# The second mixture by one level of Strassen's method, VectorE for its sums, explicit orders, and new attention orders

## The chip, the cores and the metric

The kernel runs on one core of a Trainium2 chip. Such a core has five engines that work side by side from their own queues: TensorE (PE: matmuls, with PEld for the loads of stationary tiles), VectorE (DVE), ScalarE (ACT), GpSimd (POOL) and SyncE (SP, here only an issuer of transfers). Matmuls write to PSUM, the rest lies in SBUF or in DRAM. The metric is the device time of one execution in microseconds.

## What is computed

Four batches (B) of 576 tokens (S), 8 heads of 64. Causal attention with a bias from a cumulative sum goes into a first mixture (a gated MLP with a spatial matrix over the tokens), and that into a second one. The second is what the change touches most.

```python
def _moe2_ref(x, mu_k, mu_r, w_k, w_v, w_r):
    x_prev = np.concatenate([np.zeros((B, 1, D)), x[:, :-1, :]], axis=1)
    xk = mu_k * x + (1.0 - mu_k) * x_prev
    xr = mu_r * x + (1.0 - mu_r) * x_prev
    k = np.maximum(xk @ w_k, 0.0)            # 512 -> 1024
    v = k * k @ w_v                          # 1024 -> 512
    r = 1.0 / (1.0 + np.exp(-(xr @ w_r)))    # 512 -> 512
    return r * v

x = attention(q, k, v, s)                    # (4, 576, 512)
h = np.maximum(x @ w_in, 0.0); u, v = h[..., :512], h[..., 512:]
gated = u * (einsum('ts,bsd->btd', w_spatial, normalize(v)) + b_spatial)
x = gated @ w_out
return _moe2_ref(x, ...)
```

The weights come as float64 and are turned into float32 on the chip.

## The kernel before

All large matmuls work on operands that are split into a high part (rounded to fp32r by a copy) and the rest (a subtraction), and take three passes into the same PSUM tile, high by high, high by rest and rest by high: the helper `three`, whose matmuls have the line L703. A split therefore costs a copy (often ScalarE, L105; on GpSimd L108, on VectorE L102) and a subtraction (L120).

*Weights.* A queue of 64 jobs decodes one tile of 128x256 each, in parts that orders name one by one: dL loads, dF (ScalarE, L132 and L133), dD (VectorE, L138 to L143, and an add on GpSimd, L145), dT (high copy on ScalarE, rest on GpSimd, into a buffer `hl`), dS stores the pair to DRAM. Fetches bring whole matrices back.

*Attention.* Sixteen pairs of heads are worked as a pipeline of steps; START is the written order of the beginning, ORDER that of each of 13 steps, TAIL1 and TAIL2 that of the end, where the first gate of mixture 1 begins. A name in them is one small piece: `xh` is the high copy of a step's queries and keys (64x1152), `s` the scores (L405), whose maxima VectorE takes (L411), `e` the transposed scores and exponentials (L443, L463), after which GpSimd cuts the diagonal (selects, L467), `a` and `b` the product with v (L501 to L505), whose sums go through DRAM and come back as `rb` to scale the output (L538).

*Mixture 1* per batch: gate u, the spatial product (L788 with `ws`, the split spatial matrix), the next batch's gate v with its normalization, projection. Vector work is put behind by `later` and `tick`, and decode steps are strewn between.

*Mixture 2* runs over 6 chunks of 384 tokens. `mix` makes the shifted mixture (VectorE L723 and L725, split by L728 and L729). `ffk` makes 8 tiles of 128 features by 384 tokens, 12 matmuls each (4 blocks of the contraction by three passes); ScalarE takes Relu out of PSUM (L983), VectorE squares (L986), ScalarE makes the high part (L987), GpSimd the rest (L990). `ffr` is the gate, three tiles of 128 tokens by 512 with 12 matmuls each; ScalarE takes exp of the negative, VectorE adds one (L1005) and takes the reciprocal (L1006). `ffv` has three tiles of 128 tokens by 512 with 24 matmuls each (the very last is done as two of 256); VectorE multiplies by the gate out of PSUM (L1018), and the tile is stored.

## Time and profile before

| | |
|---|---|
| median of 3 runs | 687.47 us (685.01 to 688.98) |
| profiled execution, span | 684.9 us |
| TensorE busy | 650.0 us, 95% of the span |
| VectorE, ScalarE, GpSimd busy | 504.3, 375.6, 341.8 us |
| granted TensorE clock, mean | 0.993 |

The span is the time from the first to the last instruction of the profiled execution, to which the views below belong; it lies 2.6 us under the median of the runs. Busy times are sums over the instructions of an engine. A matmul's shown time reaches to its modelled end, beyond the start of the next, so what a matmul costs is read from the distances between starts. What ended an idle time stands behind an arrow. The granted clock is a share of 2.4 GHz, 0.5 being 1.2 GHz.

### The profile page before, as it was taken

To read this page: it belongs to the slowest core of one execution; us is meant where nothing else is said; L and a number is where in the kernel's file an instruction comes from. 1 tells how busy PE (TensorE), PEld (TensorE's weight loads), DVE (VectorE), ACT (ScalarE), POOL (GpSimd) and SP (SyncE) were. 2 spreads that over 40 slices of the span, in tenths; PEclk is the share of its full clock that TensorE was granted. 3 is DMA by queue.
4 is the path that set the end of the run, shared out by engine and by line. 5 is a ranking of instruction groups with operands and counts; after the bars stand their busy time and mean duration, and the time that the engine had idled before them with its cause. 6 is when DMAs were issued, how large, how long until landed. Compare 5 with 4: busy or idle time off the path is not lost.

```text
span 684.9 us, 10966 instructions
## 1 busy us (share of the span) xinstructions
PE 650.0 (95%) x3640; PEld 558.0 (81%) x3640; DVE 504.3 (74%) x1038; ACT 375.6 (55%) x824; POOL 341.8 (50%) x490
## 2 busy tenths in 40 slices
PE   2599999999999979999999999999999999999998
PEld 1476666666757968998999999988989898898987
DVE  6878887878853687768858754479596877959773
ACT  5599999999975474575565453331423323142330
POOL 4445656565674646566567555442434344244430
PEclk9999999999999989999999999999999999999999
DMA  6645556564458627562364572721001010000101
GB/s 180 131 107 151 156 144 161 143 164 128 123 158 264 210 72 222 158 198 94 101 208 146 150 260 84 258 111 47 0 1 47 0 47 1 31 17 1 46 1 47
DMA packets 65065, 78.23 MB, mean 114 GB/s; under 512 B 28763, under 2 KB 45563, under 8 KB 64496
## 3 DMA queue, kind: packets, MB, share of 16 engines
q1 hardware_dynamic: 63674, 75.81, 37.0%
q10 hardware_dynamic: 1334, 1.72, 1.0%
q8 instruction: 28, 0.46, 0.3%
q14 instruction: 29, 0.24, 0.1%
...
## 4 chain that ended last, share of the span: by engine, by line
PE 78%; DMA 9%; ACT 7%; DVE 4%; issue 1%; POOL 0%; ACTq 0%; SPq 0%; DVEq 0%
PE mm L703 57%; PE mm L788 8%; PE pv L505 4%; DMA r<-pt 3%; PE ps L443 3%; DMA qk<-in_qk_dram 2%; ACT big L105 2%; ACT pt L516 2%; PE pv L502 2%; DMA rd<-r 1%; PE s L405 1%; ACT e L463 1%; PE pv L501 1%; DVE jk L411 1%; DMA big<-augd 1%
## 5 line engine op out<-in xcount | busy, mean ns | idle before, releaser
L703 PE MATMUL mm<-big 128*128 128x384 f32 (+2 forms) x1176 | 202.5, 332 | 0.0
L703 PEld LDWEIGHTS mm<-big 128*128 128x128 f32 x1176 | 191.3, 188 | 8.6
L703 PE MATMUL mm<-w,vb 128*128 128x512 f32 (+1 forms) x304 | 90.4, 381 | 0.0
L986 DVE TENSOR_TENSOR r<-r 128x384 f32<-128x384 f32 x48 | 53.7, 1119 | 46.6 <-ACT r L983 46.6
L443 PE MATMUL ps<-big 128*128 128x288 f32 (+3 forms) x320 | 84.0, 362 | 1.7 <-ACT e L463 0.8
L405 PE MATMUL s<-big 128*128 128x288 f32 (+3 forms) x192 | 61.9, 378 | 20.4 <-POOL big L108 12.3
L145 POOL TENSOR_TENSOR f<-f,raw 128x256 int32<-128x256 int32 x64 | 53.4, 834 | 43.9 <-DVE f L143 33.7
L411 DVE CUSTOM_DVE_ANT_0 jk<-s,mask 128x288 bf16<-128x288 f32 (+4 forms) x160 | 61.9, 429 | 16.2 <-PE s L405 13.9
L467 POOL TENSOR_SCALAR_AFFINE_SELECT e<-e 128x128 f32<-128x128 f32 x128 | 52.4, 419 | 42.0 <-ACT e L463 37.2
L443 PEld LDWEIGHTS ps<-big 128*128 128x128 f32 x320 | 55.3, 197 | 19.8 <-issue 12.1
L405 PEld LDWEIGHTS s<-big 128*128 128x128 f32 x192 | 36.3, 206 | 36.6 <-DVE mx L411 12.6
L463 ACT ACTIVATE e<-ps 128x288 f32<-128x288 f32 (+3 forms) x160 | 60.6, 418 | 8.5 <-PE ps L443 7.1
L703 PEld LDWEIGHTS mm<-w,vb 128*128 128x128 f32 x304 | 56.0, 188 | 11.2
L788 PE MATMUL mm<-ws,vb 128*128 128x288 f32 x384 | 59.3, 303 | 4.6 <-DVE ws L120 2.6
L505 PE MATMUL pv<-e,vp 128*65 128x448 f32 (+2 forms) x192 | 63.5, 436 | 0.0
L1006 DVE RECIPROCAL rr<-rr 128x512 f32<-128x512 f32 x18 | 60.4, 3353 | 0.6
L788 PEld LDWEIGHTS mm<-ws,vb 128*128 128x128 f32 x384 | 54.8, 194 | 5.6 <-DVE ws L120 3.4
L987 ACT CAST vb<-r 128x384 fp32r<-128x384 f32 x48 | 24.7, 515 | 56.9 <-DVE r L986 56.9
L729 POOL TENSOR_TENSOR gh<-mix,vb 128x384 fp32r<-128x384 f32 x24 | 25.5, 1070 | 52.3 <-ACT vb L728 49.7
L703 PE MATMUL mm<-gh,wo 128*128 128x288 f32 x256 | 51.3, 294 | 0.0
L729 POOL TENSOR_TENSOR big<-mix,big 128x384 fp32r<-128x384 f32 x24 | 25.9, 1083 | 47.4 <-ACT big L728 38.7
L120 DVE TENSOR_TENSOR big<-qk,big 64x1152 fp32r<-64x1152 f32 (+1 forms) x37 | 44.3, 1201 | 6.1 <-ACT big L105 4.9
...
## 6 DMA issues: line engine op xcount, KB each, us to landing
...
```

The source lines that it names most:

```text
L145: nc.gpsimd.tensor_tensor(out=f, in0=f, in1=low, op=ALU.add)
L405: nc.tensor.matmul(out=ps[:, 0:kn], lhsT=W[g][:, h, 128 * i:128 * i + 128], rhs=X[g][:, x0:x0 + kn], start=True, stop=True,)
L411: nc.vector.tensor_tensor_reduce(out=jk[r0:128, 0:kn], in0=ps[r0:128, 0:kn], in1=mask[r0:128, m0:m0 + kn], scale=1.0, scalar=(dst if mid e ...
L443: nc.tensor.matmul(out=ps[:, o:o + b - a], lhsT=st[g][:, key0(h, 128 * j):key0(h, 128 * j) + 128], rhs=mv[g][:, h, 64 + a:64 + b], start=( ...
L463: nc.scalar.activation(out=e[:, o:o + n], in_=ps[:, 0:n], func=ACTF.Exp, scale=scale)
L467: nc.gpsimd.affine_select(out=d, in_=d, pattern=[[1, w]], base=0, channel_multiplier=-1, compare_op=ALU.is_ge, fill=0.0,)
L505: nc.tensor.matmul(out=pv[0:VW, 1, 448 - w:448], lhsT=lt, rhs=e[:, OFF[j]:OFF[j] + w] if j < 4 else es[p][:, w * h:w * h + w], start=False ...
L703: nc.tensor.matmul(out=ps, lhsT=x, rhs=y, start=(m == 0), stop=(m == n - 1))
L729: nc.gpsimd.tensor_tensor(out=dst[1][:, kc, :], in0=t, in1=dst[0][:, kc, :].bitcast(F32), op=ALU.subtract)
L788: nc.tensor.matmul(out=o, lhsT=x[:, sc, dd], rhs=y[:, sc, t], start=(sc == 0 and m == 0), stop=False)
L986: nc.vector.tensor_tensor(out=r, in0=r, in1=r, op=ALU.mult)
L1006: nc.vector.reciprocal(out=r, in_=r)
```

## The change

Both layers of the second mixture, `ffk` and `ffv`, are computed by one level of Strassen's method in Winograd's form: operands are taken as 2x2 blocks, of which four sums are made on the token side, and seven products of blocks take the place of eight. The sums of the weights are made once while decoding: four blocks of a weight give seven forms (`dC`: three subtractions on VectorE and one on GpSimd), each split and stored, so that there are 88 splits and stores instead of 64, and seven forms of 1 MB per weight are fetched.

The first layer works per batch on halves of 288 tokens and in chains of two feature tiles (8 chains of 7 products of 12 matmuls of 288 columns, per tile 6). The second works on 9 chunks of 256 tokens (7 products of 12 matmuls of 256 columns). Products add up in PSUM: bank X takes P1, P6, P7, P4 one upon the other, Y takes P5 and P3, Z takes P2. After P1, P6 and P7 ScalarE copies X out, before the next product is added to it; the results C11, C12, C22 are the sum of such a copy and another bank, by VectorE (with Relu in the first layer), C21 is X itself. The first layer's results are squared (mostly ScalarE), stored to DRAM and loaded again for the second. The gate takes ScalarE's Sigmoid in place of exp, add and reciprocal, and needs a second activation table for it.

Orders are written out for all of this (M0 to M3 for mixture 1 with its decode parts, K_ORDER, K_LAST, V_ORDER), in place of `later` and `tick`. START, ORDER, TAIL1 and TAIL2 are new. In attention, the `xh` copy and the high copy of a weight go from ScalarE to GpSimd; in mixture 1 the latter is ScalarE's, and 13 of the 32 rests L796 go from GpSimd to VectorE. Of the issuers, q of pair 0 (`ldq0`) and k of pair 1 (`ldk1`) go from ScalarE to SP, one transfer (`Mb`) from SP to ScalarE. The ring of split weights has 4 buffers instead of 2.

```diff
-    START = """ldk0 ldq0 lds ldk1 cx0 mask cw0 sums 0xh0 bases cx1 ldq1 sums2 0wh0 0ul0 dL 0wh1 rx00 dL 0ul1 augd pads0
...
+    START = """lds cx0 ldk0 cw0 dL tiny 0xh0 mask sums ldq0 ldq1 dL bases pads1 sums2 pads0 1wh1 ldk1 cx1 0wh0 rx00
...
+    def dec_combine(group, to):
+
+        b11, b12, b21, b22 = group
+        t2, t3, t4 = (tsp.tile([128, WN], F32, tag="ts", name="ts") for _ in range(3))
+        subtract(ENGINE["c3"], out=t3, in0=b22, in1=b12)
+        subtract(ENGINE["c1"], out=b12, in0=b12, in1=b11)
+        subtract(ENGINE["c2"], out=t2, in0=b22, in1=b12)
+        subtract(ENGINE["c4"], out=t4, in0=b21, in1=t2)
...
+    PROD = dict(P1=("A11", "B11", "X"), P5=("S1", "T1", "Y"), P6=("S2", "T2", "X"), P2=("A12", "B21", "Z"),
+                P7=("S3", "T3", "X"), P4=("A22", "T4", "X"), P3=("S4", "B22", "Y"))
+    COPY_OF = {"P1": "p1", "P6": "u2", "P7": "u3"}
+    SUM_OF = {"C11": ("Z", "p1"), "C22": ("Y", "u3"), "C21": ("X", None), "C12": ("Y", "u2")}
...
+    def product(ch, nm, j, n, pairs):
+
+        w, bank = PROD[nm][1:]
+        if nm in ("P1", "P2", "P5"):
+            ch[bank, j] = mm_tile()[:, 0:n]
+        ps = ch[bank, j]
+        m, last_m = 0, 3 * len(pairs) - 1
+        for (ah, al), (bh, bl) in pairs:
+            for x, y in ((ah, bh), (ah, bl), (al, bh)):
+                nc.tensor.matmul(out=ps, lhsT=x, rhs=y, start=(m == 0 and nm in ("P1", "P2", "P5")),
+                                 stop=(m == last_m), skip_group_check=True)
+                m += 1
...
+        def keep(nm, j):
+            u = COPY_OF[nm]
+            ch[u, j] = KC.take()
+            nc.scalar.copy(KC.items[ch[u, j]], ch["X", j])
+
+        def give(c, j):
+            bank, u = SUM_OF[c]
+            k = ch[c, j] = KO.take()
+            o, ps = KO.items[k], ch[bank, j]
+            if u is None:
+                nc.scalar.activation(out=o, in_=ps, func=ACTF.Relu)
+                return
+            nc.vector._custom_dve(TENSOR_ADD_SAT, out=o, in0=ps, in1=KC.items[ch[u, j]], s0=float("inf"), s1=0.0)
+            KC.free[ch[u, j]] = True
...
+        def add(q):
+            bank, u = SUM_OF[q]
+            ch[q] = VO.take()
+            nc.vector.tensor_tensor(out=VO.items[ch[q]], in0=ch[bank, 0], in1=VC.items[ch[u]], op=ALU.add)
+            VC.free[ch[u]] = True
...
+        def sig(i):
+            RS[c, i] = RT.take()
+            nc.scalar.activation(out=RT.items[RS[c, i]], in_=ops["ps", i], func=ACTF.Sigmoid)
...
-        r = bt.tile([128, 512], F32, tag="vr", name="rr")
-        nc.scalar.activation(out=r, in_=ps, func=ACTF.Exp, scale=-1.0)
-
-        def sig():
-            nc.vector.tensor_scalar(out=r, in0=r, scalar1=1.0, scalar2=None, op0=ALU.add)
-            nc.vector.reciprocal(out=r, in_=r)
...
+    V_ORDER = """sa3 xp1 ncH n+1 xP5 sa0 n+3 ru0 xP6 xu2 n+2 xP2 ncS ncA x+C11 xP7 xu3 nsA sa2 n+4 sd3 rg0 x+C22 ru1
...
```

ScalarE's queue in one attention step, before (CAST rows of `big` are the splits of queries and keys, `hl0` is the high part of a weight, `e` the exponentials, `pt` the output out of PSUM):

```order
L105 CAST big_73<-qk0_137 64x2x576
L463 ACTIVATE e_1279<-ps_1280 128x288
L105 CAST big_73<-qk0_137 64x1152
L105 CAST hl0_85<-f_1153 128x256
L463 ACTIVATE e_1279<-ps_1295 128x288
L105 CAST big_73<-big_73 64x1152
L463 ACTIVATE e_1279<-ps_1323 128x448
L516 ACTIVATE pt_1337<-pv_1287,eps_142 65x576
L463 ACTIVATE e_1279<-ps_1339 128x192
L463 ACTIVATE e_1344<-ps_1345 128x288
L463 ACTIVATE e_1279<-ps_1356 128x320
L105 CAST big_73<-big_73 64x2x576
```

and after:

```order
L106 CAST big_73<-qk1_151 64x2x576
L518 ACTIVATE e_1442<-ps_1443 128x288
L518 ACTIVATE e_1442<-ps_1450 128x288
L518 ACTIVATE e_1442<-ps_1466 128x192
L518 ACTIVATE e_1480<-ps_1481 128x288
L106 CAST big_73<-big_73 64x1152
L518 ACTIVATE e_1442<-ps_1494 128x320
L571 ACTIVATE pt_1504<-pv_1462,eps_155 65x576
L518 ACTIVATE e_1442<-ps_1506 128x448
L106 CAST big_73<-big_73 64x2x576
L518 ACTIVATE e_1480<-ps_1530 128x192
```

Of the four copies of queries and keys three are left, the one from the loaded `qk` as 64x1152 is gone, and so is `hl`.

GpSimd's queue in one step, before (AFFINE_SELECT cuts the diagonal of `e`, L538 scales an output, L120 and L145 belong to the weight decode):

```order
L467 AFFINE_SELECT e_1279<-e_1279 128x128 x2
L467 AFFINE_SELECT e_1344<-e_1344 128x128
L467 AFFINE_SELECT e_1279<-e_1279 128x128
L467 AFFINE_SELECT e_1344<-e_1344 128x128 x2
L538 TENSOR_TENSOR x1_72<-pt_1171,rb_1304 64x576
L481 AFFINE_SELECT e4_1410<-e4_1410 128x128
L484 MEMSET e4_1410 64x64
L467 AFFINE_SELECT e_1344<-e_1344 128x128
L467 AFFINE_SELECT e_1445<-e_1445 128x128
L120 TENSOR_TENSOR hl1_86<-f_1319,hl1_86 128x256
```

and after:

```order
L109 TENSOR_SCALAR hl1_86<-f_1182 128x256
L121 TENSOR_TENSOR hl1_86<-f_1182,hl1_86 128x256
L522 AFFINE_SELECT e_1276<-e_1276 128x128 x2
L109 TENSOR_SCALAR big_73<-qk0_150 64x1152
L522 AFFINE_SELECT e_1314<-e_1314 128x128
L522 AFFINE_SELECT e_1276<-e_1276 128x128 x2
L147 TENSOR_TENSOR f_1348<-f_1348,raw_840 128x256
L593 TENSOR_TENSOR x1_72<-pt_1173,rb_1327 64x576
L522 AFFINE_SELECT e_1314<-e_1314 128x128 x3
```

The two copies stand here now: `hl1` ahead of its own subtraction, `qk` between two selects.

TensorE at the beginning of mixture 2, after (`mm` with a number is a PSUM tile; a chain's bank X is 5758 and 5765, Y 5772 and 5779, Z 5802 and 5809; `big` are the weights' forms, `xs` and `vb` the token side):

```order
L987 MATMUL mm_5758<-xs_5605,big_73 128x288 x6
L987 MATMUL mm_5765<-xs_5605,big_73 128x288 x6
L987 MATMUL mm_5772<-xs_5605,big_73 128x288 x6
L987 MATMUL mm_5779<-xs_5605,big_73 128x288 x6
L987 MATMUL mm_5758<-xs_5605,big_73 128x288 x6
L987 MATMUL mm_5765<-xs_5605,big_73 128x288 x6
L987 MATMUL mm_5802<-vb_2770,big_73 128x288 x6
L987 MATMUL mm_5809<-vb_2770,big_73 128x288 x6
L987 MATMUL mm_5758<-vb_2770,big_73 128x288 x6
L987 MATMUL mm_5765<-vb_2770,big_73 128x288 x6
L987 MATMUL mm_5841<-xs_5605,big_73 128x288 x6
L987 MATMUL mm_5848<-xs_5605,big_73 128x288 x6
```

The products are P1, P5, P6, P2, P7 and the next chain's P1: between two products into bank X there is one of another bank or chain. Before, eight tiles of 12 matmuls of 384 columns followed one another, each in a PSUM tile of its own.

VectorE in the second layer, before (L986 squares, `mix` rows make the mixtures, L1005 and L1006 the gate; a part of a chunk of 384 tokens):

```order
L986 TENSOR_TENSOR r<-r 128x384 x8
L723 TENSOR_SCALAR mix<-x_72,small 128x384
L725 SCALAR_TENSOR_TENSOR mix<-x_72,small,mix 128x384
L1005 TENSOR_SCALAR rr<-rr 128x512
L1006 RECIPROCAL rr<-rr 128x512
L723 TENSOR_SCALAR mix<-x_72,small 128x384
L725 SCALAR_TENSOR_TENSOR mix<-x_72,small,mix 128x384
L1005 TENSOR_SCALAR rr<-rr 128x512
```

and after, one chunk of 256 tokens (L959 from `vf` are sums and rests, L1141 adds out of PSUM, L1150 and the rows into `rt` multiply by the gate, L1176 mixes):

```order
L959 TENSOR_TENSOR vf<-vf 128x512 x3
L1141 TENSOR_TENSOR vf<-mm,vf 128x256
L959 TENSOR_TENSOR gl<-vf,gl 128x1024
L959 TENSOR_TENSOR vf<-vf 128x512
L1176 SCALAR_TENSOR_TENSOR hl_86<-x_72,small,hl_86 128x256
L1141 TENSOR_TENSOR vf<-mm,vf 128x256
L1176 SCALAR_TENSOR_TENSOR hl_86<-x_72,small,hl_86 128x256
L959 TENSOR_TENSOR rt<-vf,rt 128x256
L959 TENSOR_TENSOR vb<-vf,vb 128x1024
L1176 SCALAR_TENSOR_TENSOR hl_85<-x_72,small,hl_85 128x256
L959 TENSOR_TENSOR rt<-vf,rt 128x256
L1176 SCALAR_TENSOR_TENSOR hl_85<-x_72,small,hl_85 128x256
```

Squares and reciprocals are gone from here; sums of 512 columns, rests of 1024 and adds out of PSUM have come.

## Rows read from the trace of the kernel before

**Rows 1.** Windows by stage: busy PE, PEld, DVE, ACT, POOL; clock; DMA.
```profile
0.00:45.30 45.30, 25.08 (x100) 18.78 (x101) 35.14 (x107) 28.48 (x56) 20.03 (x53) 0.96 0.59 143
45.30:195.90 150.60, 145.50 (x782) 102.59 (x780) 123.93 (x401) 142.81 (x288) 86.70 (x169) 1.00 0.55 143
195.90:247.40 51.50, 45.24 (x249) 35.71 (x246) 28.88 (x61) 29.65 (x68) 29.67 (x45) 0.98 0.65 202
247.40:431.80 184.40, 184.40 (x1266) 178.23 (x1267) 128.55 (x252) 99.22 (x257) 109.91 (x133) 0.99 0.49 155
431.80:681.40 249.60, 249.60 (x1250) 222.73 (x1248) 187.38 (x218) 75.49 (x159) 95.44 (x92) 1.00 0.12 44
681.40:684.90 3.50, 0.15 (x2) 0.00 (x0) 0.42 (x1) 0.00 (x0) 0.00 (x0) 1.00 0.11 37
```

**Rows 2.** TensorE groups, 45.3 to 195.9: busy, mean ns, idle before.
```profile
L502 PE MATMUL pv<-e,vp 128*65 128x448 f32 x52 | 23.8, 539 | 0.0
L405 PE MATMUL s<-big 128*128 128x288 f32 x52 | 21.9, 421 | 3.0 <-DVE mx L411 2.9
```

**Rows 3.** Timeline of TensorE in one attention step: start, duration.
```profile
111.28 0.92 PE L502 MATMUL pv<-e,vp 128*65 128x448 f32 x2
```

**Rows 4.** Timeline of the start, 8.5 to 13.5.
```profile
9.42 1.32 ACTq L342 DMA_DIRECT2D big<-big  x1
12.26 1.68 PE L405 MATMUL s<-big 128*128 128x288 f32 x4 [12.26 <-POOL big L108]
```

**Rows 5.** Groups of ScalarE instructions, 45.3 to 195.9.
```profile
L105 ACT CAST big<-big 64x1152 fp32r<-64x1152 f32 x25 | 28.8, 1153 | 0.6
L105 ACT CAST big<-qk 64x1152 fp32r<-64x1152 f32 x24 | 27.6, 1152 | 2.0 <-DMA qk<-in_qk_dram 1.5
L105 ACT CAST hl<-f 128x256 fp32r<-128x256 f32 x13 | 5.3, 406 | 0.3
```

**Rows 6.** Groups of GpSimd instructions, 0 to 45.3.
```profile
L108 POOL TENSOR_SCALAR big<-big 64x576 fp32r<-64x576 f32 x5 | 3.3, 670 | 1.9 <-ACT big L105 1.8
```

**Rows 7.** Groups of VectorE instructions, 45.3 to 195.9.
```profile
L120 DVE TENSOR_TENSOR big<-qk,big 64x1152 fp32r<-64x1152 f32 x25 | 34.3, 1371 | 3.1 <-ACT big L105 2.7
```

**Rows 8.** Groups of TensorE instructions, 195.9 to 247.4.
```profile
L788 PE MATMUL mm<-ws,vb 128*128 128x288 f32 x11 | 3.3, 397 | 4.6 <-DVE ws L120 2.6 <-ACT ws L105 2.0
```

**Rows 9.** Windows of 12 us around the first spatial products.
```profile
240.00:252.00 12.00, 7.40 (x31) 6.37 (x30) 10.28 (x19) 9.62 (x21) 4.11 (x5) 0.72 0.15 50
```

**Rows 10.** Timeline of TensorE, runs of one shape in the mixtures.
```profile
340.45 12.88 PE L703 MATMUL mm<-big 128*128 128x288 f32 x96
...
431.83 16.81 PE L703 MATMUL mm<-big 128*128 128x384 f32 x96
...
672.07 0.39 PE L703 MATMUL mm<-w,big 128*128 128x512 f32 x1
...
673.45 0.39 PE L703 MATMUL mm<-w,big 128*128 128x512 f32 x1
...
675.73 0.40 PE L703 MATMUL mm<-w,vb 128*128 128x256 f32 x2
...
681.27 0.28 PE L703 MATMUL mm<-w,kl 128*128 128x256 f32 x1
```

**Rows 11.** Groups of VectorE and ScalarE instructions, 431.8 to 681.4.
```profile
L1006 DVE RECIPROCAL rr<-rr 128x512 f32<-128x512 f32 x18 | 60.4, 3353 | 0.6
L986 DVE TENSOR_TENSOR r<-r 128x384 f32<-128x384 f32 x48 | 53.7, 1119 | 46.6 <-ACT r L983 46.6
L1018 DVE TENSOR_TENSOR rr<-mm,rr 128x512 f32<-128x512 f32 x17 | 11.3, 666 | 5.0 <-PE mm L703 5.0
L1018 DVE TENSOR_TENSOR rr<-mm,rr 128x256 f32<-128x256 f32 x1 | 0.4, 425 | 2.1 <-PE mm L703 2.1
...
L806 ACT COPY x<-mm 128x288 f32<-128x288 f32 x1 | 0.4, 399 | 1.2 <-PE mm L703 1.2
```

**Rows 12.** The line that loads the activation table: count, min/median/max ns.
```profile
L62 ACT ACT_TABLE_LOAD  x1: 1283/1283/1283, 0.8 to 0.8; - x1
```

More of the change, by code (lines that the diff above doesn't have):

```diff
@@ L204, in tile_kernel @@
     fetches = []
-    def fetch_slowly(w, d, nm):
-        while n_done[0] < last[nm]:
-            dec_step()
-        for c in range(w.shape[2]):
-            fetches.append((w, d, c))
     def fetch_part():
         if fetches:
-            w, d, c = fetches.pop(0)
-            nc.sync.dma_start(out=w[:, :, c, :].bitcast(F32), in_=d[:, :, c, :])
+            w, d = fetches.pop(0)
+            nc.sync.dma_start(out=w.bitcast(F32), in_=d)
     def fetch_rest():
@@ L704, in three @@
                 m += 1
-    TN = 384
-    XK = [part_of(1, 1536 * i, 4, TN) for i in range(2)]
-    XM = {"k": XK}
     def runs(t0, n):
@@ L1021, in tile_kernel @@
[L1021 to L1038 removed]
+            for x in tail_ring:
+                ring.remove(x)
@@ new lines, in tile_kernel @@
+        for nm in (M0, M1, M2, M3)[b].split():
+            if nm == "K":
+                break
+            nm, _, eng = nm.partition(":")
+            ops.pop(nm)(eng or ("P" if nm[0] == "l" else "V")) if nm[0] not in "df" else ops[nm](eng or None)
+    need("d_w2")
+    wctx.close()
+    fctx.close()
+    c1 = pool(ctx.enter_context(ExitStack()), "c1", 1)
+    XS = c1.tile([128, 3 * 1152], F32R, name="xs")
+    VF = c1.tile([128, 8272], F32, name="vf")
+    kd = [wdram.tile([128, 8, S], F32, name=f"kd{i}") for i in range(B)]
```

608 lines of the change are left out of this document (429 added, 179 removed).

## The prediction

> **What bounds the kernel now.** I read the stages first, then inside each stage the engine that is full and what ends its waits. By stage [rows 1] the start (to 45.3 us) has TensorE at 25.08 of 45.30, with no engine full: it is latency. In the 13 repeated attention steps (45.3 to 195.9, 11.58 us each) ScalarE is busy 142.81 of 150.60 us and TensorE 145.50. The tail of attention and the first gate take 51.5 us. Mixture 1 (184.4 us) and mixture 2 (249.6 us) have TensorE busy for all of the time, at a granted clock of 0.99 and 1.00, while VectorE is at 70 and 75%, ScalarE at 54 and 30%, GpSimd at 60 and 38%. So in the mixtures what TensorE has to stream decides; in the attention steps it is ScalarE, with TensorE close behind.
>
> How close? A matmul's shown time is not its share of the engine, since the next starts before its end: two of 448 columns that show 539 ns each take 0.92 together [rows 2, 3], so they start 0.38 apart. For the window's 782 matmuls [rows 1] I took, for each kind of pair of neighbours, the distance between starts at its tenth percentile: they sum to 10.07 us per step. TensorE could therefore go 1.5 us per step faster, not more. ScalarE has 10.99 busy per step.
>
> **Start.** The first score matmul (12.26) waits for GpSimd's part and before that for rows whose transfer ScalarE issues only at 9.42 [rows 4], behind copies that wait for q. After, the transfer is issued between those copies, and q, which ScalarE had issued behind k, is issued by SP. That brings q forward by one issue at most (1.32 for one in [rows 4]), while more weight loads share DMA engines that are busy 59% there [rows 1]. Bounds -3 and +2, I take **-1.0**.
>
> **Attention steps.** ScalarE loses one copy 64x1152 (1.152) and one weight copy 128x256 (0.406) per step [rows 5]: 1.56, leaving 9.43. GpSimd gains both. Its own 64x576 copy takes 0.67 [rows 6], so 64x1152 is an estimated 1.3 (twice), and 128x256 some 0.35 (by 256 of 576 columns, with something fixed); 86.70/13 = 6.67 becomes 8.3. The causal selects stand in GpSimd's queue behind the 1.3 us copy, and the second attention product waits for them; the order shows it between two of them. A step can't get below 10.07 (TensorE) and won't get shorter than now by more than ScalarE's 1.56. Nothing gained is the other end: TensorE is idle for only (150.6 - 145.5)/13 = 0.39 per step by its shown times, and part of its idle time ends with VectorE's maxima [rows 2], not with ScalarE. I take the middle, 10.8 us, since two engines at 95 and 97% never both run full: -0.78 x 13 = **-10** (bounds 0 and -18).
>
> **Tail and first gate.** Between 240 and 252 us TensorE is busy 7.40 of 12.00, waits for the pieces of ws from VectorE and ScalarE, and its granted clock is 0.72 for the 12 us [rows 8, 9]: it falls after TensorE sat waiting. VectorE is busy 10.28 there, so this is its queue. The new order puts one weight decode less ahead of it (some 1.3 us of VectorE). If that moved the whole gap it would give 4.6 us of idle and 0.28 x 12 = 3.4 of clock; an order that is only a little shorter gives **-1.5** (bounds -4 and +2).
>
> **Mixture 1.** Nothing of TensorE changes. Added under it: 24 more splits and stores of 256 KB, 8 combines (24 VectorE and 8 GpSimd subtractions of 128x256), 14 fetches of 1 MB of which 7 fall here; 13 rests go from GpSimd to VectorE; the mixing of the first chunk goes. VectorE goes from 128.55 to some 150 of 184.4, ScalarE from 99 to 109 and GpSimd stays near 110 [rows 1]. That cover holds as long as no engine passes 184. The weakest place is the last batch, where some 13.6 MB move in 40 us: 340 GB/s against 155 on average [rows 1]. If the forms came late, the first products of mixture 2 would wait, not mixture 1. I take **+1** (bounds 0 and +6).
>
> **Mixture 2, TensorE.** The three passes stay; the product count falls from 8 to 7, and tiles get narrower, so columns per matmul matter. Pitches by runs of one shape: 288 columns 12.88/96 = 0.134, 384 columns 16.81/96 = 0.175, 512 columns (673.45 - 672.07)/6 = 0.230, 256 columns (681.27 - 675.73)/47 = 0.118 [rows 10]. All have a fresh stationary tile before each matmul, as the new ones do. First layer: 6 chunks x 8 x 12 = 576 of 384 columns, 100.9; after, 8 chains x 7 x 12 = 672 of 288, 90.2: -10.7 (one less of 384 per 1.17 of 288). Second layer: 408 of 512 and 48 of 256, 93.8 + 5.7 = 99.5; after, 9 chunks x 7 x 12 = 756 of 256, 89.1: -10.4. The gate's 216 of 512 stay. Together **-21.1 if TensorE stays fed**. Spread over 7 x (8 + 9) = 119 products, a wait of 0.18 each would eat it all.
>
> **Mixture 2, the others.** Prices: ScalarE's copy of 288 columns out of PSUM 0.399; VectorE on 512 out of PSUM 0.666, on 256 0.425 [rows 11]; on 1152 columns 1.371 (1024 then some 1.22) [rows 7].
> - K, per batch (two chains, 168 x 0.134 = 22.5 us of TensorE). ScalarE: 12 copies 4.8, 4 Relu 1.6, 14 squares about 6, 7 casts of 576 and two scalings about 6.1: 18.5, 82%. VectorE: 4 mixes, 4 sums and 4 rests on 576 columns at some 0.75, 12 adds out of PSUM at 0.45, 2 squares: 15.3, 68%. GpSimd some 5.7. A copy out of bank X must end before the next product may add to that bank; one other product (12 x 0.134 = 1.6 us) stands between, against 0.8 us of copies. So a copy is late only if ScalarE is more than 0.8 us behind, which I see at the end of a batch, where six squares and casts stand ahead: 0.3 to 0.8 per batch. I take 0.6 x 4 = 2.4.
> - V, per chunk (84 x 0.118 + 24 x 0.230 = 15.4 us of TensorE). VectorE: 4 mixes at 0.45, 4 sums on 512 at 0.67, rests of 3 x 1.22 and 0.67, 7 on 256 at 0.425: 11.8, 77%. ScalarE about 9. GpSimd two rests on 512, 2.7. The 18 reciprocals of 3.353 are gone, 60.4 us of VectorE [rows 11], replaced by ScalarE's Sigmoid. I take 0.3 x 9 = 2.7 of waits.
> - The Sigmoid needs a second activation table; the one load in the trace takes 1.283 [rows 12]. ScalarE has it behind other work and in front of PSUM copies: between 0 and 1.3, I take 0.4. The Trainium skill ("ScalarE: Activation LUTs", "What ACT_TABLE_LOAD costs") adds a drain of about 1.38 us and so 2.66 per switch; by it this line would be at most 1.4 more. In the row here the next activation starts right behind the load, which doesn't show the drain, but nothing was running before it.
> Together -21.1 + 5.5 = **-15.6** (bounds -21 and 0).
>
> **End.** Now the last matmul starts at 681.27, and 3.5 us follow it [rows 1, 10]. After, the last product leads to an add, a multiplication (0.425 each) and a store of 256 KB instead of 128: **+0.8** (0.3 to 1.5).
>
> **Sum.** -1.0 - 10 - 1.5 + 1 - 15.6 + 0.8 = -26.3, made against the profiled execution, whose span is 684.9. The median of the runs is 687.47, 2.6 over it (the runs lie between 685.01 and 688.98), so I predict 687.47 - 26.3 = **661 us**.
>
> **Rivals.**
> - *The attention steps stay at 11.4 or above.* For: TensorE shows 97% busy and GpSimd's copy stands among the selects. Against: the 1.5 us of slack that the starts show. Time: 661 + 8 to 10 = 669 to 671. Chance 0.17.
> - *Waits between products.* Bank X has only one product of cover. Should ScalarE or VectorE run 0.1 us late per product, 12 us of the 15.6 go, and with pauses long enough the clock goes too, as in [rows 9]. Time: 668 to 682, say 674. Chance 0.13.
> - *VectorE becomes the bound in V, slower than before.* Squares of 384 columns take 1.119 on VectorE with a GpSimd rest beside them [rows 11], while 512 columns out of PSUM take 0.666: some 0.545 would be expected, so it takes 2.05 times as long. If every VectorE operation of V slowed like that, a chunk would need 11.8 x 2.05 = 24.2 us instead of 15.4: +79, some 740. It decides from 15.4 + 26.3/9 = 18.3 us per chunk. Against: GpSimd works just 2.7 of 15.4 us there, so plainly VectorE comes to 11.8 + 2.7 x 0.5 = 13.2 us. Time where it decides: 690 to 740. Chance 0.06. The Trainium skill ("GPSIMD Engine Reference", "1. Specifications") says that GpSimd shares its SBUF interfaces with VectorE, with contention for instructions with two SBUF inputs. The rows of the squares agree with it; by it alone, V's two-input sums and rests would suffer, its reads from PSUM less.
> - *Better.* The steps run at TensorE's 10.2 (-18) and the gap at 240 closes (-5). Time: 648 to 651. Chance 0.13.
> - *No change that can be measured:* only if attention gains nothing and waits eat the rest. 0.03.
>
> **How the numbers follow.** The forecast itself (653 to 668) has 0.48. Faster by over 0.5% (3.4 us, about what this measurement can tell from none) are the forecast, the first rival, better and the second, 0.91 together; the same 0.03; slower 0.06. The range of 645 to 679 takes in the bounds of the steps, of mixture 1 and most of the second rival, and leaves out the third and the ends of the others, under 0.2.
>
> **What would show it.** Step period 10.6 to 11.0 by the last matmuls of a step; ScalarE near 9.4 busy per step, GpSimd near 8.3. Mixture 1 still 184 to 186. K some 91 to 95 us with pitch 0.134, V with the gate some 140 to 145. VectorE under 14 busy per V chunk. Wrong, if TensorE's waits in mixture 2 end with ScalarE's copies by more than 6 us, if the fetches of forms land after K's first product wants them, or if attention's waits end with GpSimd's copy.

## The result, and the profile after

The changed kernel takes 679.14 us (median of 4 runs, 678.33 to 679.95) against 686.60 us of the kernel before in the same measurement: a ratio of 0.9873, 95% interval 0.9849 to 0.9896. It is faster, by about 8 us where 26 were forecast. The profiled execution has a span of 676.5 us against 684.9, so the 8.4 us can be looked for stage by stage.

The windows of the changed kernel, with the columns of [rows 1]: start, twelve attention steps, the last three, from the last attention product to the first spatial product, mixture 1 from there on, mixture 2, end.

```profile
0.00:42.00 42.00, 26.71 (x107) 19.35 (x108) 34.53 (x104) 27.89 (x54) 21.20 (x54) 1.00 0.63 142
42.00:178.30 136.30, 130.88 (x725) 94.82 (x723) 119.68 (x372) 117.92 (x241) 109.70 (x178) 1.00 0.62 152
178.30:211.70 33.40, 31.14 (x159) 21.60 (x158) 18.12 (x46) 19.57 (x46) 24.03 (x45) 1.00 0.63 182
211.70:237.70 26.00, 21.47 (x136) 19.62 (x134) 15.87 (x34) 11.50 (x27) 12.78 (x14) 1.00 0.57 173
237.70:436.30 198.60, 189.99 (x1277) 181.40 (x1278) 161.84 (x311) 111.98 (x294) 123.93 (x150) 0.97 0.61 197
436.30:671.70 235.40, 232.02 (x1646) 220.22 (x1644) 163.97 (x277) 137.91 (x300) 54.00 (x34) 0.99 0.43 139
671.70:676.50 4.80, 0.23 (x2) 0.03 (x1) 0.85 (x2) 0.00 (x0) 0.00 (x0) 0.89 0.29 109
```

With the same marks in the timelines of both kernels (last attention product of the first step 46.2 and 42.0, twelve steps on 184.9 and 178.3, last of all 219.1 and 211.7, first spatial product 240.1 and 237.7, first product of mixture 2 431.8 and 436.3, last matmul 681.3 and 671.7):

| stage | before, us | after, us | change | forecast |
|---|---|---|---|---|
| start and first step | 46.2 | 42.0 | -4.1 | -1.0 |
| twelve attention steps | 138.7 | 136.2 | -2.5 | -9.4 |
| last three steps | 34.2 | 33.4 | -0.7 | in the -10 |
| from there to the first spatial product | 21.0 | 26.0 | +5.0 | -1.5 |
| first spatial product to mixture 2 | 191.8 | 198.6 | +6.9 | +1.0 |
| mixture 2 | 249.4 | 235.4 | -14.1 | -15.6 |
| after the last matmul | 3.6 | 4.9 | +1.3 | +0.8 |

Mixture 2 did nearly what was computed. The attention steps take 11.35 us where they took 11.56 and 10.8 were forecast, and 12 us were lost between the last attention product and mixture 2, where the change was thought to cost nothing. The stretches are read from starts of matmuls and rounded one by one.

**Attention.** ScalarE is down from 132.9 us in the twelve steps to 117.92, which is 9.8 a step where 9.4 were forecast, and TensorE has no fewer gaps for it. Some of the longest waits in the twelve steps follow (who waited for what: us in total, times, longest). `r` takes the row sums out of the output tile, `rd` their reciprocals to DRAM, `rb` brings these back to scale the outputs; `mt` is the row of score maxima.

```profile
POOL x L593 <- DMA rb<-rd: 13.6, 7, 3.0
DVE r L581 <- DMA r<-pt: 5.5, 7, 1.6
PE ps L498 <- DMA big<-mt: 2.6, 5, 0.7
DVE jk L466 <- PE s L460: 2.4, 7, 1.0
```

GpSimd's groups there, which answer to [rows 6]:

```profile
L593 POOL TENSOR_TENSOR x<-pt,rb 64x576 f32<-64x576 f32 x12 | 22.1, 1842 | 20.1 <-DMA rb<-rd 13.6 <-ACT e L518 6.4
L109 POOL TENSOR_SCALAR big<-qk 64x1152 fp32r<-64x1152 f32 x12 | 14.6, 1220 | 1.1
L109 POOL TENSOR_SCALAR hl<-f 128x256 fp32r<-128x256 f32 x12 | 4.8, 400 | 0.0
```

The large copy takes 1.22 us on GpSimd (1.3 estimated). GpSimd is busy 9.1 us of a step where 8.3 were forecast: its other operations became longer, the scaling L593 from 1.53 to 1.84 us and the addition of the weight decode (L147, in the old kernel L145) from 0.74 to 1.21. Its 20 us of waiting stand before the scalings, not the copies. The steps are not even: they take between 10.5 and 12.6 us. Taken at the shortest distance that each of the 60 matmuls of a step ever has to its next, a step would be 10.35 us (10.81 before). The 1.0 us above that are waits that come and go, and TensorE's listed ones are for the row of maxima (`mt`, 2.6 us) that a transfer brings, and for VectorE's maxima (2.0 us). SP, the engine that issues most transfers, waits longest in front of `rb`, which must not start before `rd` has landed:

```profile
SPq L589 <- DMA rd<-r: 25.7, 12, 2.7
```

What stands behind `rb` in SP's queue waits with it. Issuing `rd` and `rb` from another queue was not tried.

**Between attention and mixture 2.** What TensorE waited for from 212 to 300 us:

```profile
PE mm L743 <- DVE big L121: 4.5, 1, 4.5
PE mm L811 <- DVE ws L121: 3.9, 2, 2.1
PE mm L811 <- issue: 3.0, 1, 3.0
PE mm L743 <- DMA big<-d_wu: 1.6, 1, 1.6
```

Before, the same stretch had the 4.6 us of [rows 8]. The window that answers to [rows 9]:

```profile
240.00:252.00 12.00, 9.89 (x50) 9.22 (x51) 9.44 (x18) 5.96 (x14) 6.48 (x8) 0.64 0.18 66
```

The granted clock is 0.64 where it was 0.72. VectorE is busy for 9.44 us here, and for 11.04 of the 12 us from 228 to 240. Full speed was lost for 10.2 us (half speed) behind the first waits and for 3.4 us behind the second; before, for 6.8 us once. Waits of over 0.6 us between the last attention product and mixture 2 exceed a usual distance by 14.4 us, before by 5.4: 9 of the 12 us lost are waits, and the rest fits the 6.8 us more at half speed. The 3.0 us are put down to nothing by the profile; they stand in front of the first spatial product, and are gone in the run below that splits the spatial matrix in another order.

**Mixture 2.** The median distances are 0.133 us for the 288 columns of K and 0.118 for the 256 of V, as read from [rows 10]. V runs almost without a gap (0.7 us over all of it). K has lost 5.5 us, about half of it in one place, where the first sums of V are made; the timeline there:

```profile
508.97 1.24 SPq L1085 DMA_DIRECT2D vf<-kd  x2
514.74 0.62 ACT L1100 CAST big<-vf 128x512 fp32r<-128x512 f32 x1 [2.19 <-DMA vf<-kd]
514.74 1.29 DVE L959 TENSOR_TENSOR vf<-vf 128x512 f32<-128x512 f32 x2 [5.84 <-DMA vf<-kd]
515.71 1.05 PE L987 MATMUL mm<-gl,big 128*128 128x288 f32 x6 [0.84 <-ACT vf L1050]
518.15 1.13 PE L987 MATMUL mm<-xs,big 128*128 128x288 f32 x4 [1.39 <-DVE rt L1059]
```

The reload of the first layer's results, two chunks of 1 MB, is issued at 509.0 and lands at 514.7; from 511 to 515 us the transfer engines are full with it (a share of 1.04, 342 GB/s). ScalarE sits 2.19 and VectorE 5.84 us in front of it (`vf<-kd`), and behind them in their queues stand the copy and the add that free PSUM banks for the next products of K: 0.84 and 1.39 us of TensorE. Behind that the granted clock is at half speed from 518.4 to 521.8 us. This chain is read from the trace; no run tested it.

VectorE's groups in V, and below in K (the last group of each list adds out of PSUM):

```profile
L959 DVE TENSOR_TENSOR vf<-vf 128x512 f32<-128x512 f32 x32 | 22.7, 749 | 0.0
L959 DVE TENSOR_TENSOR gl<-vf,gl 128x1024 fp32r<-128x1024 f32 x6 | 7.3, 1224 | 3.5 <-ACT gl L1100 3.5
L1141 DVE TENSOR_TENSOR vf<-mm,vf 128x256 f32<-128x256 f32 x26 | 10.9, 420 | 22.9 <-PE mm L987 21.6 <-ACT vf L1136 1.3
```

```profile
L1010 DVE SCALAR_TENSOR_TENSOR vf<-x,small,vf 128x576 f32<-128x576 f32 x12 | 12.4, 1055 | 0.0
L959 DVE TENSOR_TENSOR vf<-vf 128x576 f32<-128x576 f32 x13 | 10.8, 848 | 0.2
L1059 DVE CUSTOM_DVE_ANT_0 rr<-mm,vf 128x288 f32<-128x288 f32 x16 | 6.7, 452 | 15.4 <-PE mm L987 15.4
```

### The profile page after: what moved, and what is told of

It reads as the page before. It is cut to its first block, busy times and chain, and to the rows that moved or that the text cites. A ratio compares the mean times of both kernels' runs of the same rounds, so it can differ in the third digit from the quotient of the medians.

```text
span 676.5 us, 12256 instructions
## 1 busy us (share of the span) xinstructions
PE 632.4 (93%) x4036; PEld 557.0 (82%) x4036; DVE 514.9 (76%) x1143; ACT 426.8 (63%) x957; POOL 345.6 (51%) x472
## 4 chain that ended last, share of the span: by engine, by line
PE 51%; DVE 3%; ACT 3%; POOL 2%; issue 2%; DMA 2%; POOLq 0%; ACTq 0%; DVEq 0%
PE mm L987 25%; PE mm L743 20%; PE mm L811 5%; DMA raw<-in_moe_w_k_dram 1%; POOL f L147 1%; POOL gl L121 1%; DVE vr L775 1%; DMA d_wkB<-big 1%; ACT rt L1069 0%; PE mm L813 0%; PE mm L812 0%; DVE ts L121 0%; POOL hl L121 0%; DVE g L141 0%; ACT raw L134 0%
## 5 line engine op out<-in xcount | busy, mean ns | idle before, releaser
L743 PE MATMUL mm<-big 128*128 128x288 f32 (+1 forms) x600 | 104.6, 333 | 6.3 <-DVE big L121 4.7
L743 PEld LDWEIGHTS mm<-big 128*128 128x128 f32 x600 | 92.4, 190 | 16.3 <-DVE big L121 6.0
L147 POOL TENSOR_TENSOR f<-f,raw 128x256 int32<-128x256 int32 x64 | 56.8, 888 | 42.0 <-DVE f L145 14.2
L466 DVE CUSTOM_DVE_ANT_0 jk<-s,mask 64x64 bf16<-64x64 f32 (+4 forms) x160 | 62.8, 424 | 7.9 <-PE s L460 5.4
L959 POOL TENSOR_TENSOR gh<-hl,gh 128x512 fp32r<-128x512 f32 x9 | 15.8, 1754 | 94.5 <-ACT gh L1193 94.5
L522 POOL TENSOR_SCALAR_AFFINE_SELECT e<-e 128x128 f32<-128x128 f32 x128 | 51.4, 427 | 15.0 <-ACT e L518 12.4
L743 PE MATMUL mm<-wo,gh 128*128 128x512 f32 x216 | 53.3, 394 | 0.2 <-ACT gh L1193 0.2
L987 PE MATMUL mm<-big,vb 128*128 128x256 f32 x384 | 47.9, 278 | 0.5 <-ACT vf L1136 0.5
L987 PEld LDWEIGHTS mm<-big,vb 128*128 128x128 f32 x384 | 46.6, 188 | 1.4 <-ACT vf L1136 0.7
L743 PEld LDWEIGHTS mm<-wo,gh 128*128 128x128 f32 x216 | 39.1, 188 | 8.9 <-POOL gh L959 0.5
L959 DVE TENSOR_TENSOR vf<-vf 128x512 f32<-128x512 f32 (+1 forms) x52 | 39.8, 798 | 6.1 <-DMA vf<-kd 5.8
L121 POOL TENSOR_TENSOR hl<-f,hl 128x256 fp32r<-128x256 f32 x45 | 38.5, 858 | 9.1 <-ACT hl L106 6.9
```

Source lines behind the costliest of these rows:

```text
L121: (nc.gpsimd if eng == "P" else nc.vector).tensor_tensor(op=ALU.subtract, **kw)
L147: nc.gpsimd.tensor_tensor(out=f, in0=f, in1=low, op=ALU.add)
L466: nc.vector.tensor_tensor_reduce(out=jk[r0:128, 0:kn], in0=ps[r0:128, 0:kn], in1=mask[r0:128, m0:m0 + kn], scale=1.0, scalar=(dst if mid e ...
L522: nc.gpsimd.affine_select(out=d, in_=d, pattern=[[1, w]], base=0, channel_multiplier=-1, compare_op=ALU.is_ge, fill=0.0,)
L743: nc.tensor.matmul(out=ps, lhsT=x, rhs=y, start=(m == 0), stop=(m == n - 1))
L959: (nc.gpsimd if ENGINE[key] == "P" else nc.vector).tensor_tensor(**kw)
```

## Experiments

All ran on the changed kernel with one edit, timed against the kernel before (686.6 to 687.9 us in each measurement). The step is the mean of twelve, from the timeline, as above. In the edits, `S`, `V` and `P` stand for ScalarE, VectorE and GpSimd. Five runs in which nothing of the attention changed (the changed kernel itself, and four of those below) have steps of 11.35 to 11.51 us: less than 0.15 between two runs says nothing.

### What holds the attention steps

**The large copy back on ScalarE.**

```diff
-wh="S", xh="P", ud="S"
+wh="S", xh="S", ud="S"
```

> The changed kernel with the 64x1152 copy of queries and keys back on ScalarE in each attention step; the weight copy stays on GpSimd, the order of pieces is the new one. Theory G (GpSimd holds the steps): GpSimd loses 1.22 us per step, step falls to 10.9 to 11.1, time 673 to 676. Theory Q (the row of maxima in SP's queue): GpSimd is no bound, ScalarE goes from 9.8 back to 10.9 busy per step, step 11.3 to 11.7, time 679 to 684.

The step is 11.92 us, the time 685.21 (ratio 0.9978, 0.9965 to 0.9991). TensorE's own waits in the twelve steps:

```profile
PE pv L556 <- ACT pt L571: 7.8, 12, 0.9
PE s L460 <- DVE mx L466: 1.2, 5, 0.3
PE ps L498 <- DMA big<-mt: 0.9, 3, 0.5
```

There is one bound now: every step waits 0.65 us for ScalarE's `pt`. The shift of this copy is worth 0.5 us a step. Theory G is not refuted by this run alone, since it takes 1.2 us a step from GpSimd and gives as much to ScalarE; against it stand the next run and the changed kernel's trace, where no matmul of the twelve steps is listed as waiting for GpSimd. The run also suggests that the new order by itself costs: with ScalarE loaded as in the old kernel (132.65 us in the twelve steps, before 132.91) the step is longer than 11.56. Apart from the order only the small copy, on GpSimd, and the larger ring of split weights differ there.

**The small copy back on ScalarE.**

```diff
-n30="V", dH="P", dO="P"
+n30="V", dH="S", dO="P"
```

> The changed kernel with the high copies of decoded weights back on ScalarE in attention (0.41 us per step). By the run that gave the larger copy back (0.57 us longer steps for 1.15 us of ScalarE) theory A (ScalarE still sets the steps by half of what it does) expects a step of 11.5 to 11.6, time 680 to 683. If GpSimd's queue or the port it shares with VectorE set them (theory G), step 11.0 to 11.25, time 674 to 678.

Step 11.45 us, time 679.02 (0.9878, 0.9853 to 0.9902): theory G's 11.25 is missed by more than the 0.15 between like runs, theory A's 11.5 is not. So GpSimd's 0.4 us are worth nothing here, and what ScalarE's 0.4 us cost is not clear of the noise. ScalarE does 121.82 us in the twelve steps here, 10.2 a step, and 11.05 in the run before; TensorE's waits for `pt` are no longer listed, so somewhere between the two it stops being the bound.

**The row of maxima from ScalarE's queue.**

```diff
-            queue(f"M{'ab'[h0]}" if p == 0 else "").dma_start(
+            queue(f"M{'ab'[h0]}" if p == 0 else "M").dma_start(
...
-    QUEUE = dict(lds="P",
+    QUEUE = dict(M="A", lds="P",
```

> The changed kernel, but the 2.5 KB row of score maxima (L481, big<-mt) of every step is issued from ScalarE's queue, right behind the copy that makes it, instead of SP's, where a 256 KB store and a 144 KB load of queries stand ahead of it (each some 0.6 us of issue). Theory Q (the steps of 11.35 us are held by this row: the fifth transposed score product waits up to 0.9 us for it): step falls to 10.8 to 11.0, the last attention product comes 4 to 6 us earlier, time 673 to 676. Rival G (GpSimd, with two more copies in its queue, holds the steps): step stays within 0.1 of 11.35, time 678 to 680. Rival P (TensorE itself is full at 11.35): no change either, and the wait moves to another row.

Step 11.98 us, time 688.86 (1.0017, 0.9999 to 1.0035). TensorE's wait for the row is gone, but ScalarE pays for the issue, as its timeline shows:

```profile
76.80 0.67 ACTq L481 DMA_DIRECT2D big<-mt  x1
77.52 0.44 ACT L133 ACTIVATE g<-raw 128x256 f32<-128x256 f32 x1 [0.75 <-ACT mt L480]
```

Each issue keeps ScalarE's next instruction back by 0.75 to 0.8 us, two of them by 1.5 a step. Theory Q can't be judged by this run: it took the wait away and loaded the engine that has 10 us to give.

**Less for VectorE.**

```diff
-        nc.vector.tensor_scalar(out=g, in0=g, scalar1=DEC_LO, scalar2=DEC_HI, op0=ALU.max, op1=ALU.min)
```

> The changed kernel without the first of the three VectorE operations of a weight decode (L139, the clamp of the exponents), so that small weights come out other than the reference's. It takes 0.53 us per attention step from VectorE and some 0.45 per decode later. Theory V: step 10.8 to 11.0 (by most of the 0.53), time 671 to 675. Theory T (transfers) and theory A (ScalarE): step 11.25 to 11.45, time 676 to 680.

Step 11.21 us, time 673.83 (0.9800, 0.9777 to 0.9823). The step gained 0.14 to 0.2 of 0.53, and in the last run below, with the same attention, it was 11.41: VectorE's load doesn't hold the steps. Of the 4 us that its span is shorter (672.5), 3 come from mixture 1 (below).

**The old order of the steps, with the copies on GpSimd.**

```diff
-    ORDER = """s4 s3 dT s0 x4 wh e0 lv rows e1 s6 x1 ul n2 a0 a3 e4 s8 s5 xh e5 s11 a2 vd ltv n2b e3 a1 zero dL a4
+    ORDER = """s4 s0 s3 wh zero lv s6 ul x1 e0 rows xh a0 dT n2 e1 a1 s1 n2b ltv s5 a2 s11 a3 dD vd x0 e2 s10 a4 s2 fa
...
```

> The changed kernel with the attention steps' pieces in the order of the kernel before; the two copies stay on GpSimd. Theory O (the engines' shift alone gives the gain and the order little): step 11.2 to 11.45, time 677 to 681. Rival (the old order was written for a short GpSimd queue, so that the two copies now delay its selects): step 11.6 or more, time 682 to 688. A step under 11.1 would say that the new order itself costs.

Step 11.81 us, time 683.31 (0.9933, 0.9910 to 0.9956). The rival came true in its time. Taken with the first run, the new order and the shift of the copies belong together; with either nearly alone the step is longer than the old kernel's 11.56.

**The normalization later.**

```diff
-    ... ul n2 a0 a3 e4 s8 s5 xh e5 s11 a2 vd ltv n2b e3 ... s2 s1 n31 s7 ...
+    ... ul a0 a3 e4 s8 s5 xh e5 n2 s11 a2 vd ltv e3 ... s2 s1 n2b s7 ... n30 n31
```

> The changed kernel with the normalization of a step's output later in the order: the reciprocal behind the fifth exponential instead of ahead of the first attention product, its broadcast load and both scalings later by about half a step. Theory N (VectorE sits 9.2 us and GpSimd 13.6 us of the 13 steps in front of transfers r and rb, and the maxima and selects behind them in the queue come late): these waits fall below 3 us each, step 10.8 to 11.1, time 672 to 676. Rival (the waits lie under TensorE's or ScalarE's work): step 11.3 to 11.5, time 678 to 681.

Step 11.88 us, time 685.23 (0.9961, 0.9945 to 0.9977). The waits in front of the transfers fell as meant, and others took their place:

```profile
POOL e L522 <- ACT e L518: 25.9, 27, 1.8
PE s L478 <- DVE mx L466: 10.6, 22, 1.0
```

Theory N is out as a way to a shorter step: with the reciprocal among them VectorE's maxima came late in nearly every step, and the steps were even, at 11.98 us.

**Keys and store behind the small transfers.**

```diff
-    Ma dS dF ldk b1 s10 e8 s9 e7 b2 Mb b4 fb ez x0 n1 ldq
+    Ma dF b1 s10 e8 s9 e7 b2 Mb b4 fb ez x0 n1 ldk dS ldq
```

> The changed kernel with the load of keys and the store of a weight behind the second row of maxima and the row sums in SP's queue, instead of between the first and the second row of maxima. Theory T (the steps swing between 10.5 and 12.6 us because small transfers, the row of maxima and the row sums, land late behind a load and a store of 144 to 256 KB issued just ahead of them): the waits for mt and r fall below 2 us over the 12 steps, mean step 10.8 to 11.1, time 672 to 676. Rival V (VectorE holds the steps, the late rows are only a sign of it): step within 0.15 of 11.4, time 677 to 681. A step over 11.6 would say that the keys are then late for the next step's copies.

Step 12.14 us (profiled execution 688.59), time 692.85 (1.0078, 1.0054 to 1.0102): the length of the last case named there, but not its reason, since no engine is listed as waiting for the loaded keys. TensorE's longest waits, and SP's:

```profile
PE s L460 <- DMA big<-big: 8.3, 6, 1.9
PE s L460 <- issue: 7.0, 4, 2.3
SPq L589 <- DMA rd<-r: 39.9, 12, 4.0
```

The waits for `mt` and `r` did fall as meant, to 0.2 us and to none listed. But the loads and the store now stand ahead of `rd`: from the issue of `rd` to that of `rb` pass 4.09 us on average, in the changed kernel 2.74. VectorE and GpSimd sit 20.7 and 20.8 us in front of `rb` (3.5 and 13.6 there), and the transfer `big<-big` for which TensorE waits stands behind `rb` in SP's queue. So theory T's mechanism is there, on another small transfer, and the edit only moved it.

**More traffic, one more issue, less traffic.**

```diff
+        stages.append({"dx": lambda: nc.sync.dma_start(out=spare, in_=moe2_w_k[0:128, 0:256])})
```

> The changed kernel with one more copy of 256 KB from DRAM to DRAM at the end of each attention step, which nothing waits for (some 15% more traffic, 0.6 us more of SP's queue). Theory T: small transfers land later still, step 11.6 to 12.0, time 682 to 688. Theories V and A: step within 0.15 of 11.4, time 678 to 681.

Step 11.74 us, time 683.79 (0.9953, 0.9934 to 0.9973).

```diff
-out=spare, in_=moe2_w_k[0:128, 0:256]
+out=spare[0:1, :], in_=moe2_w_k[0:1, 0:256]
```

> The changed kernel with one more transfer at the end of each attention step, as in the run with 256 KB more, but of 2 KB. Six runs with the same attention code have steps of 11.35 to 11.51. If the place in SP's queue (0.6 us) is what cost 0.3 us there, the step is 11.65 to 11.8 and the time 682 to 685; if the traffic, 11.35 to 11.5 and 678 to 681.

Step 11.45 us, time 677.40 (0.9868, 0.9835 to 0.9900). The windows of the twelve steps of the two:

```profile
42.80:183.70 140.90, 132.41 (x723) 94.81 (x722) 120.65 (x372) 118.29 (x241) 108.03 (x178) 1.00 0.62 170
```
```profile
42.35:179.70 137.35, 131.31 (x722) 94.36 (x721) 120.41 (x372) 118.23 (x241) 110.16 (x178) 1.00 0.57 151
```

The same number of issues, 170 GB/s in one and 151 in the other: the traffic costs 0.3 us a step, the place in SP's queue nothing that can be measured. The mirror of it:

```diff
-        nc.sync.dma_start(out=dst, in_=hl.bitcast(F32))
+        n = 2 if n_done[0] >= last["d_wo"] else 1
+        nc.sync.dma_start(out=dst[:, 0:n], in_=hl[:, 0:n, :].bitcast(F32))
```

> The changed kernel with the low parts of the weights of mixture 1 neither stored nor fetched (the high parts are fetched in their place, so that these weights are used in low precision): 128 KB less traffic in each attention step, the same instructions on the engines, two more issues per fetch. Theory T (traffic makes the small transfers late): step 11.15 to 11.3, time 674 to 678. If traffic has a cost only when added, or the issue had it: 11.35 to 11.5, time 678 to 681.

Step 11.36 us, time 676.19 (0.9843, 0.9804 to 0.9882): inconclusive. 128 KB less gave no shorter step than the shortest of the unchanged ones.

### What was lost between attention and mixture 2

**Without the extra decoding.**

```diff
-        subtract(ENGINE["c3"], out=t3, in0=b22, in1=b12)
...
-            (b11, "B11", 0), (b12, "T1", 0), (b21, "B21", 0), (b22, "B22", 0), (t2, "T2", 1), (t3, "T3", 1), (t4, "T4", 1)))
+            (b11, "B11", 0), (b12, "T1", 0), (b21, "B21", 0), (b22, "B22", 0)))
```

> The changed kernel without the 8 combinations of weight blocks and without 24 of the 88 splits and stores: the forms T2, T3 and T4 are read from other stored forms, all products and fetches stay. Theory D (mixture 1 and the tail lost 12 us against before because the engines beside TensorE are full of the extra decoding): from the first spatial product to the first Strassen product 198.6 us falls to 192 to 194, time 671 to 675. Rival C (the loss lies ahead of the extra work, in the order of pieces around 234 to 265 us and in the clock that falls after it): 197 or more, time 677 to 680.

Time 678.00 (0.9867, 0.9841 to 0.9892), first spatial product to mixture 2 197.4 us: rival C. The combinations and the 24 further splits cost about 1 us.

**The spatial matrix in the order of its use.** In the edit `p0` to `p4` are the blocks' high copies, with an `s` behind the name their rests.

```diff
-    dS dF p3 ... p3s p1 q5 q6 dF p0 p2 q7 g4r p0s p2s g2r dL B0 dD dD p4 p1s dF ...
+    dS dF p0 ... p0s p1 q5 q6 dF p2 p3 q7 p1s p2s p3s g4r g2r dL B0 dD dD p4 dF ...
```

> The changed kernel with the splits of the spatial matrix in the order in which the first spatial product reads them (blocks 0, 1, 2, 3 ahead of the held half block and of the bias rows). Theory W (the 3.0, 1.75 and 2.1 us that TensorE waits between 234 and 243 us are VectorE and ScalarE coming to blocks 0 and 1 too late in their queues): the waits fall to under 2.5 us together, and the clock stays at full speed for longer, -4 to -8 us, time 671 to 675. Rival: VectorE is simply full there (9.4 of 12 us busy), another piece is then late (the rest of v or the bias) and the waits stay above 5 us, time 677 to 680.

Time 680.19 (0.9902, 0.9887 to 0.9917). The rival: the waits for `ws` shrink, and a wait for v's half block takes their place.

```profile
PE mm L811 <- DVE vb L121: 4.8, 1, 4.8
PE mm L743 <- DVE big L121: 4.4, 1, 4.4
PE mm L811 <- DVE ws L121: 2.7, 2, 1.4
```

**The second batch's x ahead of the fetch of w_out.** In the edit `x` and `y` are copies and rests of that x, `W` is the fetch.

```diff
-    ... y2 x1 dT ... y1 dT:V ... dC dD W x3 dC s01 ... s21 h21 y0 l21 dL y3:P dD ...
+    ... y2 x1 x3 dT ... y1 y0 y3 dT:V ... dC dD W dC s01 ... s21 h21 l21 dL dD ...
```

> The changed kernel with the copy of the last block and the rests of two blocks of the second batch's x moved ahead of the fetch of w_out in the first batch's order, the last rest from GpSimd to VectorE. Theory B (that fetch forces a burst of decoding, behind which the operands of the next gate come 4.5 us too late at 260 us): the wait falls below 1 us and with it the fall of the clock after it, -4 to -6 us, time 673 to 675. Rival: the engines are full of decode work for the whole stage, so that the wait comes back a few us later at another operand, time 677 to 680.

Time 679.26 (0.9897, 0.9877 to 0.9917). The trace is of an execution of 686.1 us, so only its places of waiting are read. The 4.5 us at 260 are gone, and waits came at 277, for the fetch of w_out, and at 291, for a ScalarE copy out of PSUM: the rival.

**And the fetch itself later.**

```diff
-    ... dC dD W dC s01 ... v1 a1 c0 r0 ...
+    ... dC dD dC s01 ... v1 a1 W c0 r0 ...
```

> The run with the second batch's x early, and the fetch of w_out behind the second tile of the next gate instead of ahead of the fifth spatial product, so that no decoding is forced ahead of the gate's operands. Theory B2 (the forced burst of decoding and the 2 MB fetch in the middle of it are the cause of the waits at 260, 277 and 291 us): no wait over 1 us between 250 and 300, time 672 to 675. Rival (decode work as a whole is too much for the first batch): the wait comes back at the first projection, time 677 to 681.

Time 698.89 (1.0168, 1.0149 to 1.0186), the slowest of all. TensorE's waits in the first batch, and then at the beginning of mixture 2:

```profile
PE mm L743 <- DMA wo<-d_wo: 4.6, 2, 2.8
```

```profile
PE mm L987 <- issue: 6.3, 1, 6.3
PE mm L743 <- POOL gl L121: 3.7, 1, 3.7
```

The rival, and worse: w_out was late for the first projection, and the decoding that had been pushed back was missing at the end of mixture 1: SP still issued stores of decoded forms at 448 us, and the first Strassen product started at 451, after 6.3 us for which the profile names no releaser. That the late decoding caused them is our reading. The way from the first spatial product to mixture 2 took 211.6 us.

**Both: without the clamp, and x early.**

> The run without the clamp together with the second batch's x moved ahead of the fetch of w_out. Theory (VectorE's queue holds the operands of the next gate; with 0.45 us less per decode the moved rests no longer push another piece late): no wait over 2 us between 250 and 295, time 668 to 671. Rival (ScalarE's queue in front of a raw load and the 2 MB fetch hold the first batch then): the wait comes back at 270 to 290, time 673 to 675.

Time 674.89 (0.9832, 0.9798 to 0.9867), no better than without the clamp alone. The waits that came back:

```profile
PE mm L742 <- ACT x L830: 2.9, 1, 2.9
PE mm L742 <- DMA wo<-d_wo: 1.6, 1, 1.6
```

The fetch of w_out is late, and ScalarE's queue holds the copy L830 that frees PSUM: the time and the place of the rival. But what ScalarE itself waits for, just ahead of that copy, is VectorE's normalization:

```profile
287.13 0.62 ACT L777 CAST vb<-vr 128x512 fp32r<-128x512 f32 x1 [2.54 <-DVE vr L774]
```

So VectorE is not cleared by this run. What VectorE's relief is worth is seen in the run without the clamp and with the old places, by the window of mixture 1:

```profile
236.50:432.20 195.70, 188.30 (x1277) 180.49 (x1278) 144.85 (x269) 112.96 (x296) 123.97 (x149) 0.97 0.61 200
```

195.7 us instead of 198.6, and from the last attention product to mixture 2 221.5 instead of 224.6. A part of the 3 us is the clock, at half speed for 6.8 us behind the first waits instead of 10.2; the wait for the rest of x stays, at 4.2 us.

**A version that beats both** is thus the run without the clamp: 673.83 us, 2.0% under the kernel before. By the clamp's bounds in the kernel it holds for weights that lie in float32's normal range; the clamp is there for those outside. Leaving the clamp out of the kernel before was not tried.

## Why the prediction was wrong

The sign was right, the size was not: -8 for -26, and 679.14 us lies just outside of the range of 645 to 679. Of the 18 us that the profiled spans show missing, 12.4 lie between attention and mixture 2 and 6.8 in the attention steps; the start gave 3.1 more than forecast. By its steps:

- *Start, -1.0:* -4.1. The first score product came 0.9 us earlier (11.38), as said; the rest is that TensorE has fewer waits up to the first step's end, and no fall of the clock there (before, 0.96 over the start [rows 1], now 1.00). This size was off in the good direction; it was not tested alone, and that it came out well is luck.
- *Attention steps, -10:* -3. **The step that failed** is "I take the middle, 10.8 us". Its lower bound, 10.07, pooled distances of like pairs at different places of the step; position by position the kernel before gives 10.81, as much as was forecast for the new step, and the changed one 10.35. And the middle stood for nothing: ScalarE did bind (0.5 us a step when its copy comes back), but the gain ends after about half of what was taken from it, somewhere between 11.05 and 10.2 us of ScalarE a step. What holds the remaining 1.0 us was only in part found. No engine's load by itself was seen to: 0.4 us moved from GpSimd to ScalarE, and 0.5 less of VectorE, changed the step by at most 0.2. More traffic lengthens it (0.3 us for 256 KB), less did not visibly shorten it; each of the three changes of the order made it longer, one of them because loads then stood ahead of `rd`. Which order or transfer would give the 10.35 stays open.
- *Tail, -1.5, and mixture 1, +1:* +5.0 and +6.9, together the largest miss. The failed step is that cover was read from busy shares: "that cover holds as long as no engine passes 184". VectorE went to 161.84 of 198.6 us, 81%, though for 11.04 of the 12 us ahead of 240, and the extra work is in fact nearly free (about 1 us in the run without it). What cost was place in the queues: pieces of ws, one rest of x and the fetch of the gate's weights (d_wu) came 1.6 to 4.5 us late in the 50 us in which one product hands over to the next, and the clock fell to half behind the waits at 234 to 243 and behind the one at 260. That place is the cause is shown for ws and x, where a new place removed the wait or shortened it; no edit of places shortened the whole, since another wait came each time. The forecast priced the gap by one weight decode; no stretch of the order behind it was followed.
- *Mixture 2, -15.6:* -14.1, **right**, by its own terms: the pitches 0.133 and 0.118 (0.134 and 0.118), waits and clock 7.0 (5.5). Within that, V's waits were 0.7 for 2.7, and K's 5.5 for 2.4, since the reload of the first layer's results was not thought of. The table's load took 1.283 us and the first Sigmoid stood 0.5 us behind it, waiting for TensorE; of the further drain of about 1.38 us of which the Trainium skill speaks ("ScalarE: Activation LUTs", "What ACT_TABLE_LOAD costs") this trace shows nothing.
- *VectorE slowed by GpSimd:* refuted as the bound of V, where VectorE took in all 10.5 us a chunk (11.8 expected). The slowing itself is there. Sorted in the trace by whether a GpSimd instruction runs beside them (none, or for over half of the time), rests of 576 columns into `vb` in K took 0.75 and 1.26 us on average (2 and 5 of them), mixes 0.81 and 1.30 (4 and 6), sums of 512 columns in V 0.68 and 0.92 (19 and 9), multiplications of 256 columns into `rt` 0.42 and 0.74 (11 and 4); adds out of PSUM kept to 0.45 in K and 0.42 in V, beside GpSimd too. So the forecast's 0.75 was right for an undisturbed instruction, and the means of 0.85 to 1.11 in the rows hold the disturbed ones. That agrees with the rule of the Trainium skill that the prediction named ("GPSIMD Engine Reference", "1. Specifications"), by which instructions with two SBUF inputs contend. It is not so for each of them: seven rests `gh` of 512 columns took 0.685 beside GpSimd as well. K had the room for it.
- *The rivals:* "the attention steps stay" was the nearest, and came true, with steps of 11.35 to 11.51 us over the runs, together with a loss ahead of mixture 2 that no rival named. It had stood at 0.17. None of the three signs of being wrong showed: TensorE's listed waits for ScalarE in mixture 2 come to 1.5 us, none is for a fetch of forms, and none in attention for GpSimd.
